# The second MLP's output product with w_out stationary and 512 tokens moving, its rows brought back by block transposes and a DRAM tile, and an earlier first plan

## The chip, the cores and the metric

One core of a Trainium2 chip. The metric is the device time of one execution in microseconds (us). TensorE is called PE here, VectorE DVE, ScalarE ACT, GpSimd POOL, and SyncE, whose only work is DMA, SP.

## What is computed

Attention with squared ReLU, times u; then a mixture of 8 experts in which each token goes to one; then a second MLP with ELU. Sizes: 8 x 3072 tokens of 256; expert hidden width 1024; hidden width of the second MLP 2048.

```python
scores = (1.0 / S) * np.matmul(z, z.transpose(0, 2, 1))
x = (u * np.matmul(np.maximum(scores, 0.0) ** 2, v)).reshape(B * S, D)
# experts
xn, en = x / norm(x), expert_emb / norm(expert_emb)
logits = xn @ en.T / tau
expert_idx, gate_w = argmax(logits, axis=1), softmax(logits) at that index
for e in range(E):
    mask = expert_idx == e
    out[mask] = gate_w[mask, None] * (np.maximum(x[mask] @ w1[e], 0.0) @ w2[e])
# second MLP, on these rows
h = x @ w_in
g = np.where(h > 0.0, h, np.exp(np.minimum(h, 0.0)) - 1.0)
return (g @ w_out).astype(np.float32)
```

## The kernel before

Each operand of a product is held as two numbers, hi and lo (a rounded part and the rest). A product is hi by hi, hi by lo and lo by hi, three matmuls for one.

**Stages.** A list of steps runs over the whole program. Its first 576 are attention: 48 chunks of 512 queries, 12 steps each. Behind them come units: A (one tile of 512 tokens of one expert, 4 steps, 41 of them), B (a rest tile of 256 tokens, 2 steps, 21), M (the second MLP on the tile of an A, 8 steps, 41), and D (the second MLP on 512 of the rows that the B units left, 8 steps, 7, the last of them by functions of its own, l_h and l_acc). Their order is A0, A1, M0, A2, M1, ... M5, then A6, B0, M6, A7, B1, M7, ..., then the remaining A and M, then D0 to D6.

**The loop over steps** (from L1343) writes for step n: its first product h on PE, the DVE operations d1 to d4 of step n - 1 with at most one planned task between two of them, the list `pre[n]` (among others the PE transposes of the next unit's rows, L852), the second product acc of step n - 2 on PE (LAG is 2), g of step n on ACT, and then the rest of the tasks planned for n. An engine runs what is written for it in that order. Tasks are placed by `at(step, task)` and `spread(tasks, first, last)`, which chooses steps by a running sum of each engine's costs.

**Buffers.** PSUM has two tiles for first products (pss, from t_ps) and two for sums (psa, from t_acc). 48 equal slots in SBUF, tag "g", hold nearly all tiles, in turn.

**The second product of M and D** is m_acc: the 128 x 128 pieces of hi and lo of g are stationary, and w_out moves: 512 wide (its hi and lo side by side) for hi, 256 wide for lo. A step has 16 matmuls. The sum of a unit takes both psa tiles, [tokens, hi-part | lo-part] for four quarters of 128 tokens. The last step goes by halves of the tokens; behind each half ACT copies the two parts to o2 and o. m_out then adds them on DVE (in-place in o) and scatters four times 128 rows to the output by the token numbers in ids, planned by the lines at L1336 to L1338.

**Attention's second product**, att_acc, is written the other way: v is stationary, 512 queries move, and psa holds the transposed result. evac_ops brings it back: a DVE transpose of 32 x 32 blocks from PSUM into xt (the columns of v are permuted by the host for that, in layout), four writes to a DRAM tile xr, one read from it as rows x.

**The plan.** route_ops counts the tokens of each expert by groups of two chunks and scatters token numbers into the table tok on POOL. plan1 works out which expert and which place in tok the first 6 A tiles have, when the group g1 (L1279) is through; plan2 does it for the rest, when all are. From those numbers POOL gathers for each unit ids from tok, then the rows of x by ids, and the weights wst by the expert.

Of the kernel before, what the change touches and what calls it, by code (L numbers as in the profile page):

```python
# [17 lines left out]
LAG = 2  # L18
# [10 lines left out]
def attn_moe_mlp(ctx, tc, zT, u, v, emb, tau, wp, w_in, w_out, out):  # L29
# [23 lines left out]

    xs = dr.tile([N, D], F32, name="xs")
    xr = dr.tile([N, D], F32, name="xr")
    tok = dr.tile([E * N, 1], I32, name="tok")
    dn = dr.tile([NR, D], F32, name="dn")
    dnid = dr.tile([NR, 1], I32, name="dnid")
# [41 lines left out]
    def cp(o, a):  # L100
        act.activation(out=o, in_=a, func=AF.Copy)  # L101
# [298 lines left out]
        tt(lo, r, f(hi), ALU.subtract)  # L400
        HL[C, m] = [hi, lo]

    def att_acc(C, m):

        if m == 0:
            AC[C] = t_acc()
        hi, lo = HL.pop((C, m))
        vt = V[C // NC, m]
        for part in range(2):
            for dc in range(2):  # L410
                a = AC[C][:, dc]
                for j in range(2):
                    vh, vl = (vt[:, j, o + dc * 128:o + dc * 128 + 128] for o in (0, 256))
                    if part == 0:
                        mm(a, vh, hi[:, j], m == 0 == j, False)
                        mm(a, vl, hi[:, j], False, False)
                    else:
                        mm(a, vh, lo[:, j], False, m == CS - 1 and j == 1)

    def evac_ops(C):  # L420

        g, o = chunk_group[C]
        h = {}
        rows = xr[C * 512:(C + 1) * 512, :]

        def tr():
            h["t"] = slot("xt", F32, (16, 2, 32))
            vec.transpose(out=h["t"], in_=AC.pop(C).rearrange("p a (b r) -> p b a r", r=32))

        def put():  # L430
            for i in range(4):
                sp.dma_start(rows.rearrange("(b r) d -> r b d", r=32)[:, :, i * 64:(i + 1) * 64],
                             h["t"][i * 32:(i + 1) * 32].rearrange("p b a c -> p b (a c)"))

        def get():
            X[C] = slot("x", F32, (4, 256))
            sp.dma_start(X[C], rows.rearrange("(t p) d -> p t d", p=128))

        def mul():
            if o == 0:  # L440
                n2t[g] = sb.tile([128, MAXT], F32, name="n2", tag="n2", bufs=3)
                dott[g] = sb.tile([128, MAXT, E], F32, name="dot", tag="dot", bufs=3)
            tt(X[C], X[C], UT.pop(C), ALU.mult)

        def sq(q):
            def fn():
                act.activation(out=K["junka"], in_=X[C][:, q], func=AF.Square,
                               accum_out=n2t[g][:, o + q:o + q + 1])
            return fn
        return tr, put, get, mul, [sq(q) for q in range(4)]  # L450
# [370 lines left out]
    def rows_ops(key):  # L821
        kind, j = key
        nt = 4 if kind == "A" else 2

        def idx(t):
            if kind == "A":
                return K["ixa"][:, j, t:t + 1] if j < NA1 else K["ixb"][:, j - NA1, t:t + 1]
            return K["ixB"][:, j, t:t + 1]
        h = {}

        def gi(t):
            def fn():
                if t == 0:
                    IDS[key] = sb.tile([128, 4], I32, name="ids", tag="ids", bufs=6)
                    h["x"] = slot("rows", F32, (4, 256))
                gather(IDS[key][:, t:t + 1], tok[:, :], idx(t), E * N - 1)
            return fn

        def gx(t):
            def fn():  # L840
                gather(h["x"][:, t], xs[:, :], IDS[key][:, t:t + 1], N - 1)
            return fn
        return [gi(t) for t in range(nt)] + [gx(t) for t in range(nt)], h
# [46 lines left out]

    def a_acc(key, i):
        if i == 0:
            AC[key] = [t_acc()[:, 0] for _ in range(2)]
        hi, lo = HL.pop((key, i))
        w = W2[key, i]
        last = i == 3
        for dc in range(2):
            a = AC[key][dc]
            for g in range(2):
                sl = slice(g * 256 + dc * 128, g * 256 + dc * 128 + 128)  # L900
                mm(a, w[:, 0, sl], hi[:, g], i == 0 and g == 0, False)
# [27 lines left out]
                scatter(dn[:, :], x[:, t], iv, NR - 1)  # L929

    PR = set()

    def m_r(key, i):
        p, e, y = PS[key, i]
# [42 lines left out]
    def l_acc(key, i):  # L977
# [14 lines left out]
                    mm(a[:, q, :256], lo[:, j, c], w[:, g, :256], False, st)  # L992
        if last:
            if hf == 0:
                PS[key] = slot("o", F32, (4, 256)), None
            o = PS[key][0][:, 2 * hf:2 * hf + 2]
            cp(o, a[:, :, 256:])
            tt(o, o, a[:, :, :256], ALU.add)
            for fn in m_out(key)[1 + 2 * hf:3 + 2 * hf]:
                fn()  # L1000

    def m_g(key, i):
        p, e, y = PS[key, i]
# [24 lines left out]

    def m_acc(key, i):
        if i == 0:  # L1030
            AC[key] = [t_acc(), t_acc()]
        hi, lo = HL.pop((key, i))
        w = WO[i]
        last = i == NF2 // 2 - 1
        for qs in ((0, 1), (2, 3)) if last else ((0, 1, 2, 3),):
            for part in range(2):
                for q in qs:
                    a = AC[key][q // 2][:, q % 2]
                    sl = slice(q * 128, q * 128 + 128)
                    for j in range(2):  # L1040
                        st = last and j == 1
                        if part == 0:
                            mm(a, hi[:, j, sl], w[:, j], i == 0 and j == 0, st)
                        else:
                            mm(a[:, :256], lo[:, j, sl], w[:, j, :256], False, st)
            if last:
                q = qs[1]
                if q == 1:
                    PS[key] = slot("o", F32, (4, 256)), slot("o2", F32, (4, 256))
                o, t = PS[key]  # L1050
                ap = AC[key][q // 2]
                cp(t[:, q - 1:q + 1], ap[:, :, 256:])
                cp(o[:, q - 1:q + 1], ap[:, :, :256])

    def m_out(key):
        def add():
            o, t = PS[key]
            tt(o, o, t, ALU.add)

        def sc(q):  # L1060
            def fn():
                ids = IDS["A", key[1]] if key[0] == "M" else IDS[key]
                scatter(out[:, :], PS[key][0][:, q], ids[:, q:q + 1], N - 1)
            return fn
        return [add] + [sc(q) for q in range(4)]

    def d_prep(key):
        h = {}

        def ld():  # L1070
            h["x"] = slot("xd", F32, (4, 256))
            IDS[key] = sb.tile([128, 4], I32, name="ids", tag="ids", bufs=6)
            j = key[1]
            sp.dma_start(h["x"], dn[j * 512:(j + 1) * 512, :].rearrange("(t p) d -> p t d", p=128))
            sp.dma_start(IDS[key], dnid[j * 512:(j + 1) * 512, :].rearrange("(t p) o -> p (t o)", p=128))
# [200 lines left out]
        route_end[g] = w  # L1276

    at(CS, plan_const)
    g1 = chunk_group[(B - 1) * NC + 1][0]  # L1279
    w = route_end[g1]  # L1280
    spread(plan1_ops(), w + 1, w + 6, 0.2)
    p1 = w + 6
# [16 lines left out]
    for un in units:  # L1299
# [34 lines left out]
            at(n - 5, dl)  # L1334
            pre[n - 2] += do
        if k in "MD" and un != units[-1]:  # L1336
            w = n + nst[k] + LAG + (2 if k == "D" else 0)
            spread(m_out(un), w, w + 2)  # L1338

    def emit(n, k):  # L1340
        if 0 <= n < len(steps):
# [21 lines left out]
def layout(u, v, z, emb, tau, w1, w2, w_in, w_out):  # L1363
# [2 lines left out]
    E, D, F = w1.shape  # L1366
    c = np.ascontiguousarray

    B, S, _ = v.shape
    vp = v.reshape(B, S, 4, 2, 32).transpose(0, 1, 3, 2, 4).reshape(B, S, D)  # L1370
    w1p = w1.reshape(E, 2, 128, F)
    w2p = w2.reshape(E, F // 128, 128, D).transpose(0, 2, 1, 3)
    return {
# [1 line left out]
        "tau": c(np.asarray(tau).reshape(1)),  # L1375
        "wp0": c(w1p[:, 0].reshape(E * 128, F)), "wp1": c(w1p[:, 1].reshape(E * 128, F)),
        "wp2": c(w2p[:, :, 0:4].reshape(E * 128, 4 * D)), "wp3": c(w2p[:, :, 4:8].reshape(E * 128, 4 * D)),
        "w_in": c(w_in).view(np.int64), "w_out": c(w_out).view(np.int64),
    }


# [15 lines left out]
```

## Time and profile before

| | us |
|---|---|
| median of 3 runs | 5435.11 |
| lowest, highest | 5433.26, 5435.74 |
| the profiled execution | 5439.36 |
| its span in the profile | 5437.4 |

The profile shows one execution. Its page gives the busy time of each engine over the span; the rows further below are from its trace. A row of the timeline is: start in us, busy time in us, engine, line, operation, the tile written and the tiles read, shape, number of instructions in the row; in brackets the idle time of the engine before it and what ended that. Busy times of matmuls overlap, so the spacing of starts is what a stream costs. A releaser is inferred from semaphores: of several it is the one that came last.

### The profile page before, as it was taken

Reading aid. Unit: us, or ns where it says so; the run is one execution under the profiler, and the core shown is the slowest. Engines: PE = TensorE matmul, PEld = TensorE weight load, DVE = VectorE, ACT = ScalarE, POOL = GpSimd, SP = SyncE. Lnnn points to the kernel's source line nnn. Section 1 sums busy time; section 2 is a strip of 40 time slices with the busy share of each in tenths; the row PEclk is TensorE's granted clock in tenths of the full one; section 3 lists DMA queues with packets and bytes.
Section 4 is the critical chain, followed back from the end, with each engine's and each line's share of the span. In section 5 each row is a group of like instructions: output and inputs, shape, how many; then the busy total and the mean of one; then the engine's idle time right before and its main releaser. Section 6 shows DMA issues by size and latency. Waiting matters only on the chain. (4 is left out here: it accounts for less than half of the span.)

```text
span 5437.4 us, 72993 instructions
## 1 busy us (share of the span) xinstructions
PE 5403.8 (99%) x26532; PEld 4566.6 (84%) x26532; DVE 4187.9 (77%) x7839; ACT 4082.3 (75%) x4762; POOL 1382.3 (25%) x1207
## 2 busy tenths in 40 slices
PE   9999999999999999999999999999999999999998
PEld 7888888888888887888888888888888888888887
DVE  8888888888888877887677667767766777777887
ACT  7989988898999885667666666666665666666776
POOL 0011101111110104324444344434444222221011
PEclk9999999999999999999999999999999999999999
DMA  3333323332333314102222222222222111110000
GB/s 112 84 79 87 83 79 86 70 90 78 82 86 83 79 53 155 55 28 74 76 68 82 65 82 66 82 68 75 74 74 70 39 52 49 48 48 27 20 24 20
DMA packets 303063, 374.11 MB, mean 69 GB/s; under 512 B 136492, under 2 KB 244527, under 8 KB 302704
## 3 DMA queue, kind: packets, MB, share of 16 engines
q0 software_dynamic: 76896, 206.62, 12.4%
q1 hardware_dynamic: 225808, 162.84, 11.6%
q8 instruction: 209, 3.42, 0.3%
q14 instruction: 150, 1.23, 0.1%
HBM read 266.72 MB, written 92.39 MB: 66 GB/s over the span
## 5 line engine op out<-in xcount | busy, mean ns | idle before, releaser
L104 PE MATMUL psa<-hi,v 128*128 128x512 f32 x4608 | 1143.8, 390 | 0.0
L104 PEld LDWEIGHTS psa<-hi,v 128*128 128x128 f32 x4608 | 865.3, 188 | 179.6 <-DVE hi L391 0.9
L83 DVE TENSOR_TENSOR lo<-r,hi 128x1024 fp32r<-128x1024 f32 x576 | 705.0, 1224 | 243.0 <-ACT hi L101 237.6
L104 PE MATMUL pss<-x2h,wi 128*128 128x512 f32 x2624 | 814.1, 391 | 0.0
L104 PE MATMUL psa<-wo,hi 128*128 128x512 f32 x3072 | 780.8, 392 | 0.6 <-DVE hi L1020 0.6
L93 DVE SCALAR_TENSOR_TENSOR y<-e,y 128x1024 f32<-128x1024 f32 x384 | 469.6, 1223 | 378.7 <-ACT e L1005 375.1
L370 ACT ACTIVATE r<-pss 128x1024 f32<-128x1024 f32 x576 | 591.1, 1026 | 207.1 <-PE pss L104 203.9
L952 ACT ACTIVATE e<-pss 128x1024 f32<-128x1024 f32 x376 | 386.5, 1028 | 430.2 <-PE pss L104 426.3
L104 PEld LDWEIGHTS psa<-wo,hi 128*128 128x128 f32 x3072 | 570.9, 188 | 115.3 <-DVE hi L1020 0.9
L375 ACT ACTIVATE r<-r 128x1024 f32<-128x1024 f32 x576 | 611.6, 1062 | 18.3
L577 POOL DMA_INDIRECT tok<-idt,pi x192 | 226.5, 1179 | 1566.0 <-DVE pi L556 860.4
L104 PE MATMUL psa<-lo,v 128*128 128x512 f32 x2304 | 615.9, 389 | 0.0
L788 POOL DMA_INDIRECT out<-o,ids x192 | 206.1, 1074 | 1567.8 <-ACT hi L879 558.2
L95 DVE SCALAR_TENSOR_TENSOR junk<-x,en 128x256 f32<-128x256 f32 x1536 | 599.8, 416 | 0.0
L879 ACT ACTIVATE hi<-pss 128x1024 fp32r<-128x1024 f32 x206 | 211.9, 1029 | 495.8 <-PE pss L104 495.8
L104 PEld LDWEIGHTS pss<-x2h,wi 128*128 128x128 f32 x2624 | 476.5, 189 | 86.4
L104 PE MATMUL pss<-x2l,wi 128*128 128x512 f32 x1312 | 510.5, 389 | 0.0
L104 PEld LDWEIGHTS psa<-lo,v 128*128 128x128 f32 x2304 | 432.7, 188 | 90.0
L101 ACT ACTIVATE hi<-r 128x1024 fp32r<-128x1024 f32 x460 | 488.3, 1062 | 14.6
L83 DVE TENSOR_TENSOR y<-r,y 128x1024 f32<-128x1024 f32 x384 | 470.6, 1225 | 33.2 <-DVE y L93 0.5
L83 DVE TENSOR_TENSOR lo<-y,hi 128x1024 fp32r<-128x1024 f32 x384 | 470.5, 1225 | 17.8
L104 PE MATMUL pss<-zp 128*128 128x512 f32 x1152 | 450.5, 391 | 14.0 <-ACT r L370 7.6
(166 smaller groups left out, 9915.7 us busy)
## 6 DMA issues: line engine op xcount, KB each, us to landing
vs<-v SPq DMA_DIRECT2D x48, 512.0 KB, 6.1
u<-u SPq DMA_DIRECT2D x48, 512.0 KB, 6.0
xr<-xt SPq DMA_DIRECT2D x192, 128.0 KB, 2.6
x<-xr SPq DMA_DIRECT2D x48, 512.0 KB, 4.9
xs<-x SPq DMA_DIRECT2D x48, 512.0 KB, 4.8
zz<-zT SPq DMA_DIRECT2D x46, 256.0 KB, 5.8
zq<-zp POOLq DMA_DIRECT2D x46, 256.0 KB, 3.9
w<-w_in SPq DMA_DIRECT2D x8, 512.0 KB, 4.3
```

Source lines behind the costliest of these rows:

```text
L83: vec.tensor_tensor(out=o, in0=a, in1=b, op=op)
L93: vec.scalar_tensor_tensor(out=o, in0=a, scalar=s, in1=b, op0=op0, op1=op1)
L95: vec.scalar_tensor_tensor(out=o, in0=a, scalar=s, in1=b, op0=op0, op1=op1, accum_out=acc)
L101: act.activation(out=o, in_=a, func=AF.Copy)
L104: pe.matmul(o, lhsT=l, rhs=r, start=start, stop=stop, skip_group_check=True)
L370: act.activation(out=r, in_=p, func=AF.Relu, scale=1.0 / S)
L375: act.activation(out=r, in_=r, func=AF.Square)
L577: pool.indirect_dma_start(out=tok[:, :], out_offset=bass.IndirectOffsetOnAxis(ap=h["pi"][:, t:t + 1], axis=0), in_=K["idt"][:, gt:gt + 1], ...
L788: pool.indirect_dma_start(out=dst, out_offset=bass.IndirectOffsetOnAxis(ap=idx, axis=0), in_=src, in_offset=None, bounds_check=bound, oob_ ...
L879: act.activation(out=hi, in_=p, func=AF.Relu)
L952: act.activation(out=e, in_=p, func=AF.Relu, scale=-1.0)
```

## The change

1. m_acc uses vw_acc, the former body of att_acc: w_out stationary, 512 tokens moving, 8 matmuls with hi and 4 with lo in a step, all 512 wide, and one psa tile for a unit in place of two. No split of the last step.
2. m_out is replaced by out_ops: the transpose, the four writes and the read of evac_ops (now rows_by_dram) with a new DRAM tile orow, then the four scatters. For a unit that starts at step n and has 8 steps: transpose in step n + 9, writes n + 10, read n + 11, scatters from n + 13 to n + 15. The ids live longer and get 8 buffers in place of 6.
3. The columns of w_out are permuted by the host as those of v are. l_acc, the last D unit's, undoes that with permuted views in its copies and additions, now by quarters of the tokens.
4. a_acc takes one psa tile where it took halves of two.
5. g1 is the group of chunk 41, not of chunk 43: plan1 goes from steps 561 to 566 into 537 to 542.

```diff
@@ -53,6 +53,7 @@
 
     xs = dr.tile([N, D], F32, name="xs")
     xr = dr.tile([N, D], F32, name="xr")
+    orow = dr.tile([N, D], F32, name="orow")
     tok = dr.tile([E * N, 1], I32, name="tok")
     dn = dr.tile([NR, D], F32, name="dn")
     dnid = dr.tile([NR, 1], I32, name="dnid")
@@ -400,32 +401,25 @@
         tt(lo, r, f(hi), ALU.subtract)
         HL[C, m] = [hi, lo]
 
-    def att_acc(C, m):
-
-        if m == 0:
-            AC[C] = t_acc()
-        hi, lo = HL.pop((C, m))
-        vt = V[C // NC, m]
+    def vw_acc(a, w, hi, lo, first, last):
+
         for part in range(2):
             for dc in range(2):
-                a = AC[C][:, dc]
                 for j in range(2):
-                    vh, vl = (vt[:, j, o + dc * 128:o + dc * 128 + 128] for o in (0, 256))
+                    wh, wl = (w[:, j, o + dc * 128:o + dc * 128 + 128] for o in (0, 256))
                     if part == 0:
-                        mm(a, vh, hi[:, j], m == 0 == j, False)
-                        mm(a, vl, hi[:, j], False, False)
+                        mm(a[:, dc], wh, hi[:, j], first and j == 0, False)
+                        mm(a[:, dc], wl, hi[:, j], False, False)
                     else:
-                        mm(a, vh, lo[:, j], False, m == CS - 1 and j == 1)
-
-    def evac_ops(C):
-
-        g, o = chunk_group[C]
+                        mm(a[:, dc], wh, lo[:, j], False, last and j == 1)
+
+    def rows_by_dram(rows, acc, get_tile):
+
         h = {}
-        rows = xr[C * 512:(C + 1) * 512, :]
 
         def tr():
             h["t"] = slot("xt", F32, (16, 2, 32))
-            vec.transpose(out=h["t"], in_=AC.pop(C).rearrange("p a (b r) -> p b a r", r=32))
+            vec.transpose(out=h["t"], in_=acc().rearrange("p a (b r) -> p b a r", r=32))
 
         def put():
             for i in range(4):
@@ -433,8 +427,21 @@
                              h["t"][i * 32:(i + 1) * 32].rearrange("p b a c -> p b (a c)"))
 
         def get():
+            sp.dma_start(get_tile(), rows.rearrange("(t p) d -> p t d", p=128))
+        return tr, put, get
+
+    def att_acc(C, m):
+        if m == 0:
+            AC[C] = t_acc()
+        vw_acc(AC[C], V[C // NC, m], *HL.pop((C, m)), m == 0, m == CS - 1)
+
+    def evac_ops(C):
+
+        g, o = chunk_group[C]
+        def x_tile():
             X[C] = slot("x", F32, (4, 256))
-            sp.dma_start(X[C], rows.rearrange("(t p) d -> p t d", p=128))
+            return X[C]
+        tr, put, get = rows_by_dram(xr[C * 512:(C + 1) * 512, :], lambda: AC.pop(C), x_tile)
 
         def mul():
             if o == 0:
@@ -831,7 +838,7 @@
         def gi(t):
             def fn():
                 if t == 0:
-                    IDS[key] = sb.tile([128, 4], I32, name="ids", tag="ids", bufs=6)
+                    IDS[key] = sb.tile([128, 4], I32, name="ids", tag="ids", bufs=8)
                     h["x"] = slot("rows", F32, (4, 256))
                 gather(IDS[key][:, t:t + 1], tok[:, :], idx(t), E * N - 1)
             return fn
@@ -890,12 +897,12 @@
 
     def a_acc(key, i):
         if i == 0:
-            AC[key] = [t_acc()[:, 0] for _ in range(2)]
+            AC[key] = t_acc()
         hi, lo = HL.pop((key, i))
         w = W2[key, i]
         last = i == 3
         for dc in range(2):
-            a = AC[key][dc]
+            a = AC[key][:, dc]
             for g in range(2):
                 sl = slice(g * 256 + dc * 128, g * 256 + dc * 128 + 128)
                 mm(a, w[:, 0, sl], hi[:, g], i == 0 and g == 0, False)
@@ -929,6 +936,7 @@
                 scatter(dn[:, :], x[:, t], iv, NR - 1)
 
     PR = set()
+    OUTS = {}
 
     def m_r(key, i):
         p, e, y = PS[key, i]
@@ -992,12 +1000,13 @@
                     mm(a[:, q, :256], lo[:, j, c], w[:, g, :256], False, st)
         if last:
             if hf == 0:
-                PS[key] = slot("o", F32, (4, 256)), None
-            o = PS[key][0][:, 2 * hf:2 * hf + 2]
-            cp(o, a[:, :, 256:])
-            tt(o, o, a[:, :, :256], ALU.add)
-            for fn in m_out(key)[1 + 2 * hf:3 + 2 * hf]:
-                fn()
+                PS[key] = slot("o", F32, (4, 256))
+            for q in range(2):
+                o = PS[key][:, 2 * hf + q]
+                ov = o.rearrange("p (i b c) -> p b i c", i=4, b=2)
+                cp(ov, a[:, q, 256:].rearrange("p (b i c) -> p b i c", i=4, b=2))
+                tt(ov, ov, a[:, q, :256].rearrange("p (b i c) -> p b i c", i=4, b=2), ALU.add)
+                scatter(out[:, :], o, IDS[key][:, 2 * hf + q:2 * hf + q + 1], N - 1)
 
     def m_g(key, i):
         p, e, y = PS[key, i]
@@ -1028,48 +1037,31 @@
 
     def m_acc(key, i):
         if i == 0:
-            AC[key] = [t_acc(), t_acc()]
-        hi, lo = HL.pop((key, i))
-        w = WO[i]
-        last = i == NF2 // 2 - 1
-        for qs in ((0, 1), (2, 3)) if last else ((0, 1, 2, 3),):
-            for part in range(2):
-                for q in qs:
-                    a = AC[key][q // 2][:, q % 2]
-                    sl = slice(q * 128, q * 128 + 128)
-                    for j in range(2):
-                        st = last and j == 1
-                        if part == 0:
-                            mm(a, hi[:, j, sl], w[:, j], i == 0 and j == 0, st)
-                        else:
-                            mm(a[:, :256], lo[:, j, sl], w[:, j, :256], False, st)
-            if last:
-                q = qs[1]
-                if q == 1:
-                    PS[key] = slot("o", F32, (4, 256)), slot("o2", F32, (4, 256))
-                o, t = PS[key]
-                ap = AC[key][q // 2]
-                cp(t[:, q - 1:q + 1], ap[:, :, 256:])
-                cp(o[:, q - 1:q + 1], ap[:, :, :256])
-
-    def m_out(key):
-        def add():
-            o, t = PS[key]
-            tt(o, o, t, ALU.add)
+            AC[key] = t_acc()
+        vw_acc(AC[key], WO[i], *HL.pop((key, i)), i == 0, i == NF2 // 2 - 1)
+
+    def out_ops(key):
+
+        i = OUTS.setdefault(key, len(OUTS))
+        h = {}
+
+        def tile_():
+            h["o"] = slot("o", F32, (4, 256))
+            return h["o"]
 
         def sc(q):
             def fn():
                 ids = IDS["A", key[1]] if key[0] == "M" else IDS[key]
-                scatter(out[:, :], PS[key][0][:, q], ids[:, q:q + 1], N - 1)
-            return fn
-        return [add] + [sc(q) for q in range(4)]
+                scatter(out[:, :], h["o"][:, q], ids[:, q:q + 1], N - 1)
+            return fn
+        return rows_by_dram(orow[i * 512:(i + 1) * 512, :], lambda: AC.pop(key), tile_) + tuple(sc(q) for q in range(4))
 
     def d_prep(key):
         h = {}
 
         def ld():
             h["x"] = slot("xd", F32, (4, 256))
-            IDS[key] = sb.tile([128, 4], I32, name="ids", tag="ids", bufs=6)
+            IDS[key] = sb.tile([128, 4], I32, name="ids", tag="ids", bufs=8)
             j = key[1]
             sp.dma_start(h["x"], dn[j * 512:(j + 1) * 512, :].rearrange("(t p) d -> p t d", p=128))
             sp.dma_start(IDS[key], dnid[j * 512:(j + 1) * 512, :].rearrange("(t p) o -> p (t o)", p=128))
@@ -1276,7 +1268,7 @@
         route_end[g] = w
 
     at(CS, plan_const)
-    g1 = chunk_group[(B - 1) * NC + 1][0]
+    g1 = chunk_group[(B - 1) * NC - 1][0]
     w = route_end[g1]
     spread(plan1_ops(), w + 1, w + 6, 0.2)
     p1 = w + 6
@@ -1334,8 +1326,12 @@
             at(n - 5, dl)
             pre[n - 2] += do
         if k in "MD" and un != units[-1]:
-            w = n + nst[k] + LAG + (2 if k == "D" else 0)
-            spread(m_out(un), w, w + 2)
+            w = n + nst[k] + LAG - 1
+            tr, put, get, *sc = out_ops(un)
+            at(w, tr)
+            at(w + 1, put)
+            at(w + 2, get)
+            spread(sc, w + 4, w + 6)
 
     def emit(n, k):
         if 0 <= n < len(steps):
@@ -1366,8 +1362,7 @@
     E, D, F = w1.shape
     c = np.ascontiguousarray
 
-    B, S, _ = v.shape
-    vp = v.reshape(B, S, 4, 2, 32).transpose(0, 1, 3, 2, 4).reshape(B, S, D)
+    vp, op = (t.reshape(-1, 4, 2, 32).transpose(0, 2, 1, 3).reshape(t.shape) for t in (v, w_out))
     w1p = w1.reshape(E, 2, 128, F)
     w2p = w2.reshape(E, F // 128, 128, D).transpose(0, 2, 1, 3)
     return {
@@ -1375,7 +1370,7 @@
         "tau": c(np.asarray(tau).reshape(1)),
         "wp0": c(w1p[:, 0].reshape(E * 128, F)), "wp1": c(w1p[:, 1].reshape(E * 128, F)),
         "wp2": c(w2p[:, :, 0:4].reshape(E * 128, 4 * D)), "wp3": c(w2p[:, :, 4:8].reshape(E * 128, 4 * D)),
-        "w_in": c(w_in).view(np.int64), "w_out": c(w_out).view(np.int64),
+        "w_in": c(w_in).view(np.int64), "w_out": c(op).view(np.int64),
     }
 
 
```

On PE, inside an M unit, a step of before (psa is the sum, pss the first product, wo and wi are w_out and w_in, x2h and x2l the expert's rows in two parts):

```order
L104 MATMUL pss<-x2l,wi 128x512
L104 MATMUL psa<-wo,hi 128x512 x8
L104 MATMUL psa<-wo,lo 128x256 x8
L104 MATMUL pss<-x2h,wi 128x512 x2
L104 MATMUL pss<-x2l,wi 128x512
```

and the same place now:

```order
L105 MATMUL pss<-x2l,wi 128x512
L105 MATMUL psa<-hi,wo 128x512 x8
L105 MATMUL psa<-lo,wo 128x512 x4
L105 MATMUL pss<-x2h,wi 128x512 x2
L105 MATMUL pss<-x2l,wi 128x512
```

Eight matmuls of 256 have become four of 512; the first product around them stands as it did.

On DVE, from the last step of an M unit into the A unit behind it (lo from pss and hi is the A unit's, one a step; w is a part of a weight, xb the rows of the next B tile, o the output rows), before:

```order
L83 TENSOR_TENSOR lo<-y,hi 128x1024
L93 SCALAR_TENSOR_TENSOR lo<-pss,hi 128x1024
L83 TENSOR_TENSOR w<-wst,w 128x512 x3
L93 SCALAR_TENSOR_TENSOR lo<-pss,hi 128x1024
L83 TENSOR_TENSOR w<-wst,w 128x512
L83 TENSOR_TENSOR xb<-pss,xb 128x512
L83 TENSOR_TENSOR o<-o,o_37142 128x1024
L93 SCALAR_TENSOR_TENSOR lo<-pss,hi 128x1024
```

and now:

```order
L84 TENSOR_TENSOR lo<-y,hi 128x1024
L94 SCALAR_TENSOR_TENSOR lo<-pss,hi 128x1024
L84 TENSOR_TENSOR w<-wst,w 128x512 x3
L422 STREAM_TRANSPOSE xt<-psa 128x1024
L94 SCALAR_TENSOR_TENSOR lo<-pss,hi 128x1024
L84 TENSOR_TENSOR w<-wst,w 128x512
L84 TENSOR_TENSOR xb<-pss,xb 128x512
L94 SCALAR_TENSOR_TENSOR lo<-pss,hi 128x1024
```

The transpose stands ahead of the A unit's second lo, where the addition stood two operations behind it.

On POOL, around the last eight scatters of token numbers (tok; ids, rows and wst are the gathers for one A unit, out the scatters of M's output rows), before:

```order
L788 DMA out<-o,ids 24576x256
L783 DMA wst<-wp,wia 128x1024
L788 DMA out<-o,ids 24576x256
L783 DMA wst<-wp,wia 128x1024 x2
L577 DMA tok<-idt,pi 196608x1 x8
L783 DMA ids<-tok,ixa 128x1 x4
L783 DMA rows<-xs,ids 128x256 x4
```

and now:

```order
L790 DMA rows<-xs,ids 128x256 x4
L790 DMA wst<-wp,wia 128x1024 x4
L584 DMA tok<-idt,pi 196608x1 x8
L795 DMA out<-o,ids 24576x256 x4
L790 DMA ids<-tok,ixa 128x1 x4
L790 DMA rows<-xs,ids 128x256 x4
```

The output scatters, which stood between the weight gathers, stand behind the token scatters.

## Rows read from the trace of the kernel before

**Rows 1.** Windows: start:end, length, busy of PE, PEld, DVE, ACT, POOL, clock, DMA, GB/s

```profile
2300.00:5200.00 2900.00, 2900.00 (x15171) 2488.40 (x15170) 2108.87 (x2210) 1949.72 (x2287) 1018.89 (x852) 1.00 0.19 60
...
2090.00:2100.00 10.00, 8.43 (x25) 6.51 (x26) 8.70 (x15) 9.91 (x17) 8.02 (x7) 0.64 0.28 92
2260.00:2270.00 10.00, 9.96 (x47) 8.44 (x48) 7.27 (x8) 4.87 (x5) 0.00 (x0) 0.83 0.00 0
```

**Rows 2.** Timeline of PE, one unit of eight D steps

```profile
5024.24 1.98 PE L104 MATMUL psa<-wo,hi 128*128 128x512 f32 x8
5026.06 1.12 PE L104 MATMUL psa<-wo,lo 128*128 128x256 f32 x8
5027.01 0.63 PE L104 MATMUL pss<-x2h,wi 128*128 128x512 f32 x2
...
5057.32 1.98 PE L104 MATMUL psa<-wo,hi 128*128 128x512 f32 x8
...
5068.38 1.98 PE L104 MATMUL psa<-wo,hi 128*128 128x512 f32 x8
```

**Rows 3.** Timeline of PE, A steps: first matmul of h, and five steps later

```profile
2128.35 0.62 PE L104 MATMUL pss<-xh,w 128*128 128x512 f32 x2
...
2155.55 0.62 PE L104 MATMUL pss<-x2h,wi 128*128 128x512 f32 x2
```

**Rows 4.** Groups by line and shape, DVE: count, busy us, mean ns, idle before

```profile
L428 DVE STREAM_TRANSPOSE xt<-psa 128x1024 f32<-128x1024 f32 x48 | 59.9, 1249 | 83.2 <-PE psa L104 83.1
L83 DVE TENSOR_TENSOR o<-o,o 128x1024 f32<-128x1024 f32 x47 | 57.2, 1216 | 0.0
```

**Rows 5.** DMA issues of the page: queue, count, KB each, us to landing

```profile
xr<-xt SPq DMA_DIRECT2D x192, 128.0 KB, 2.6
x<-xr SPq DMA_DIRECT2D x48, 512.0 KB, 4.9
```

**Rows 6.** Timeline of DVE, PE and ACT, an A unit behind M, B next

```profile
3389.39 1.23 DVE L93 SCALAR_TENSOR_TENSOR lo<-pss,hi 128x1024 fp32r<-128x1024 f32 x1 [1.36 <-ACT hi L879]
...
3390.91 0.63 PE L104 MATMUL pss<-xh,w 128*128 128x512 f32 x2
...
3391.11 1.09 ACT L101 ACTIVATE o<-psa 128x512 f32<-128x512 f32 x2 [0.31 <-PE psa L104]
...
3393.69 0.46 PE L852 MATMUL pss<-ident,rows 128*128 128x128 f32 x4
```

**Rows 7.** Timeline of DVE and POOL at the last eight token scatters

```profile
2286.22 0.17 DVE L556 CAST pi<-sm 128x8 int32<-128x8 f32 x1
...
2299.59 1.34 POOL L577 DMA_INDIRECT tok<-idt,pi  x1 [0.30 <-issue]
...
2335.11 1.73 POOL L783 DMA_INDIRECT ids<-tok,ixa  x1 [3.56 <-DMA tok<-idt,pi]
...
2335.96 0.70 DVE L1020 CAST hi<-y 128x1024 fp32r<-128x1024 f32 x1
```

**Rows 8.** Timeline of POOL, ACT and PE where the stages meet

```profile
2071.80 1.06 POOL L783 DMA_INDIRECT ids<-tok,ixa  x1 [4.98 <-DVE junk L95]
...
2088.01 0.63 ACT L101 ACTIVATE w<-wst 128x512 fp32r<-128x512 f32 x1 [10.77 <-DMA wst<-wp,wia]
...
2091.57 0.80 PE L104 MATMUL pss<-zp 128*128 128x512 f32 x1 [7.61 <-ACT r L370]
...
2260.04 0.88 PE L852 MATMUL pss<-ident,rows 128*128 128x128 f32 x8 [1.96 <-ACT r L937]
```

**Rows 9.** Timeline of POOL and DVE at the end

```profile
5399.11 1.21 POOL L788 DMA_INDIRECT out<-o,ids  x1 [34.62 <-ACT r L937]
...
5403.79 0.69 DVE L83 TENSOR_TENSOR o<-o,psa 128x512 f32<-128x512 f32 x1 [0.93 <-ACT o L101]
...
5416.14 0.97 POOL L788 DMA_INDIRECT out<-o,ids  x1 [1.70 <-DMA out<-o,ids]
...
5424.06 0.97 POOL L788 DMA_INDIRECT out<-o,ids  x1 [6.95 <-DVE o L83]
```

## The prediction

> **What bounds the kernel now.** I read the table of windows first: from 2300 to 5200 us, the stage of the experts and of the second MLP, PE is busy for 2900.00 of 2900.00 us at a granted clock of 1.00 (2.4 GHz), while DVE has 2108.87 and ACT 1949.72 us of work [rows 1]. So there the time is what PE issues, and anything else matters only if it makes PE wait. Second, PE's timeline, for the distance between the starts of two pieces of its stream; busy durations overlap and can't be added. Third, the timelines of DVE, ACT and POOL at the few places where PE is closest to a wait. PE did wait where the stages meet: 7.61 us before 2091.57 and 1.96 us before 2260.04 [rows 8], each followed by a stretch of low clock (0.64 and 0.83 [rows 1]).
>
> **The stream of PE in an M or D unit.** One of the 8 steps has 12 matmuls of h, 512 wide, then in m_acc 8 with hi, 512 wide, and 8 with lo, 256 wide [rows 2]. In numbers of that piece: 5026.06 - 5024.24 = 1.82 us for the eight hi, 5027.01 - 5026.06 = 0.95 us for the eight lo, and the rest of the step for h. Six steps last 5057.32 - 5024.24 = 33.08 us, 5.513 each, and the unit of eight 5068.38 - 5024.24 = 44.14 us; its last step, cut in two halves of tokens, is only a little longer.
> After: 8 hi and 4 lo, all 512 wide. The columns are the same (8 x 256 = 4 x 512); four issues fewer. The row nearest to the new step is an A step, which has 12 matmuls of h and 12 of the second product, all 512 wide and with the weights stationary, as the new m_acc has them: five such steps last 2155.55 - 2128.35 = 27.20 us, 5.440 each [rows 3]. The new unit is thus 8 x 5.440 = 43.52 us, and the saving 44.14 - 43.52 = 0.62 us a unit. There are 41 M units and 7 D units, of which the last keeps its own path (l_acc): 47 x 0.62 = **29.1 us**, all of it on the path that sets the end. Bounds: 0, if the new step took 5.513 like the old, and 29.1; I take the A steps, since operand form, width and count are equal. Where the 0.62 lies: by the A steps a matmul of 512 columns is 5.440/24 = 0.2267 us, so in each old step the lo pairs are 0.95 - 4 x 0.2267 = 0.043 too long (four pairs, 11 ns each, 1504 pairs, 16 us in all), and h and hi together 5.513 - 0.95 - 20 x 0.2267 = 0.03; eight such steps are 0.58, the split of the last step the remaining 0.04.
>
> A rule bears on this. The Trainium skill, "TensorE: Matmul & The Clock Gate", section "Back-to-back issue gap", gives an isolated matmul of N columns at the full clock N/2.4 ns plus 2.5 ns. By it two matmuls of 256 cost only 2.5 ns more than one of 512, and my estimate from that page is 1504 x 2.5 = 3.8 us instead of 29.1. The trace's 11 ns a pair, and its steps, speak against it; the case is a rival below, with a price from rows.
>
> **The evacuation.** Gone per unit: four ACT copies from PSUM and a DVE addition (1.216 us, 47 of them [rows 4]). New: one DVE transpose from PSUM, for which the attention's of the same shape is the row (1.249 us [rows 4]). DVE's work is equal within 0.03 us a unit, ACT's falls; neither engine sets the end [rows 1]. The detour over DRAM adds, per unit, four writes of 128 KB and a read of 512 KB, in attention 2.6 and 4.9 us to landing [rows 5]. They are issued by SP a step apart; the four scatters come two steps behind the read, 2 x 5.44 = 10.9 us against 4.9. Behind them on POOL stand gathers for tiles several steps ahead. On SP the read stands ahead of the D units' loads, which are made five steps early. Cost 0; without that cover POOL would hold its queue for the rest of a landing, at most 4.9 us, still less than a step. IDS gets 8 buffers for the longer life of the ids.
>
> **The transpose at the head of the A units.** This is the new dependence I looked at most. In the order of DVE the transpose stands ahead of the second lo(A). In before, lo(A) of the first step runs at 3389.39 for 1.23 us, and PE's transposes for the B tile (L852), which want the PSUM buffer that lo(A) reads, start at 3393.69 [rows 6]: 3.07 us of margin. After, DVE first waits for the end of m_acc's last step: in before the next matmul starts at 3390.91 and ACT's copy 0.20 us later, at 3391.11 [rows 6]. With m_acc 0.06 shorter the transpose would run from 3391.05 to 3392.30, lo(A) directly behind it to about 3393.45, and PE wants the buffer at about 3393.6. A margin of 0.1 to 0.2 us, in each of the 21 places where A, B and M follow one another. Bounds: 0, and 0.3 us each (the two operations without any overlap and a hand-over of 0.20 between them and to PE: 3391.05 + 1.25 + 0.20 + 1.23 + 0.20 = 3393.93): 6.3 us. I take 0.5 us in total, as the times close without a wait.
>
> **M1 and the token scatters.** On POOL M1's four output scatters stood ahead of the last group's eight token scatters; now they stand behind. In before these run from 2299.59 to 2335.11, 35.5 us, though their index was written at 2286.22 already [rows 7]; now they may start as soon as that is there and the four weight gathers are issued. If they start at 2286.4 the outputs go at about 2322 to 2334, if at 2299.6 at 2335 to 2347. The slot of that o tile is used again by a hi (2335.96 [rows 7]), on which PE depends about 4 us later. Bounds 0 and 4 us, once; I take 0.5.
>
> **The earlier plan.** The six first A tiles are planned 24 steps earlier, from 42 chunks. But the stall between the stages ends with a transfer: ACT's w waits 10.77 us for the weight gather and PE 7.61 us for ACT's r behind it [rows 8]. On POOL the eight token scatters of group 21 still stand ahead of the ids gather (2071.80 [rows 8]), and that gather still reads the token table, so it waits for the last of them to land; row and weight gathers follow as before. The row names a DVE operation (junk) as releaser, but by the code the ids gather needs of DVE only its index tile, which plan1 wrote steps earlier. I take 0; the bounds are 0 and the whole stall, 7.61 us plus the low clock behind it, 10 x (1 - 0.64) = 3.6 us: 11.2 us gained.
>
> **The tail.** In before D5's four scatters and the first pair of the last unit are six, from 5399.11 to 5416.14, 3.41 us apart; the last pair goes at 5424.06, as its o is done [rows 9]. Now the first pair goes first (its o is done at 5403.79 + 0.69 [rows 9]), then D5's four: six scatters to 5404.5 + 6 x 3.41 = 5425.0 in the old frame, 0.9 later than 5424.06; at 2.7 us apart no delay, at 3.9 apart 3.8. Each token quarter's o is scattered by itself, which may gain 0.5. Bounds -0.5 and +3.8; I take +0.5.
>
> **Sum:** -29.1 + 0.5 + 0.5 + 0 + 0.5 = **-27.6 us**. The profiled execution took 5439.36 us; with the change 5411.8. The median of three runs is 4.2 us below it, 5435.11; with the change **5407.5 us** (-0.5%).
>
> **Rivals.**
> *Part of it comes back.* The margin of A's lo is negative (6.3 us), and M1's slot (4) and the tail (3.8) go towards their upper bounds: 5435.11 - 29.1 + 6.3 = 5412 with the first alone, 5420 with all. For it: margins of 0.1 us in 21 places. Against it: PE follows DVE and ACT closely elsewhere, with a window of 2900 us without idle time [rows 1].
> *The stall between the stages shrinks.* Then 11.2 us more go: 5407.5 - 11.2 = 5396.3. For it: plan operations leave DVE just there. Against it: the transfer chain above.
> *The change does not do what it says for PE.* The surcharge isn't the narrow matmul's but something that stays (the switch between operands, the first reading of hi). Then the step stays at 5.513 us, the 29.1 us are not there and the terms above add 1.5: 5435.11 + 1.5 = 5436.6, no change. Against it: the A steps [rows 3]. The Trainium skill's rule cited above would give the same case with 3.8 us less, 5432.8.
> *Slower.* lo(A) behind the transpose makes PE wait long enough in each of the 21 places for the clock to fall, as the wait of 1.96 us before 2260.04 did [rows 8], which was followed by 10 us at 0.83, 1.7 us lost [rows 1]. 21 x (1.96 + 1.7) = 77 us against 27.6: 5435.11 - 27.6 + 77 = 5484. It decides from 27.6/21 = 1.3 us per place, wait and clock together, which is a DVE delayed by about one more operation of 1.2 us than I count.
>
> **Chances.** Forecast 0.61, part of it comes back 0.17, smaller stall 0.09, no change 0.08, slower 0.05. A measurement of this kernel can tell about 0.2%, 11 us, from no change: forecast, part and smaller stall are beyond that, faster 0.87, same 0.08, slower 0.05. The range reaches from 5399 (a third of the stall gone beside the sum) to 5423 (the upper end of the part that comes back, 5420, and the 2.5 us by which the runs before differ): it leaves out the whole stall gone, no change and slower, 0.22 in all, with a little of the stall's case inside.
>
> **What would show it.** Right: in a unit in the late D stage the start-to-start of a step is 5.44 us and of a unit 43.5; the matmul rows lose the 256-wide lo of m_acc; 48 + 47 transposes of about 1.25 us; DVE's additions of 128x1024 o are gone; PE's waits still hold about 7.6 us for r and 2 us at the second place, and nothing new of over 10 us in sum. Wrong: steps of 5.5 us (the surcharge stays); PE waiting for DVE's lo at the L852 transposes 21 times; a clock below 1.00 in windows of the A, B, M cycles; POOL waiting for reads of x rows' kind for steps; a stall between the stages shorter or longer than before.

## The result, and the profile after

The changed kernel takes 5486.86 us (median of 4 runs, 5481.33 to 5488.64), the kernel before 5435.42 us in the same comparison: a ratio of 1.0093, 95% interval 1.0076 to 1.0111. It is 51 us slower (41 to 60 by the interval), where 28 us faster was forecast.

The first part of the page (busy us of each engine, share of the span, instructions), of the kernel before and then, with its span, of the changed kernel; the span before is 5437.4 us:

```profile
PE 5403.8 (99%) x26532; PEld 4566.6 (84%) x26532; DVE 4187.9 (77%) x7839; ACT 4082.3 (75%) x4762; POOL 1382.3 (25%) x1207
```

```profile
span 5479.4 us, 70218 instructions
...
PE 5385.4 (98%) x25028; PEld 4483.5 (82%) x25028; DVE 4189.4 (76%) x7841; ACT 3982.2 (73%) x4576; POOL 1404.0 (26%) x1207
```

1504 matmuls are gone, and PE has less to do over the whole span, yet the span is longer. So PE waits. The table of windows for the stretch of [rows 1] says how long (length, then busy time of PE, PEld, DVE, ACT, POOL, clock, DMA share, GB/s):

```profile
2300.00:5200.00 2900.00, 2841.16 (x13655) 2380.24 (x13654) 2069.66 (x2175) 1830.46 (x2094) 1036.86 (x849) 1.00 0.24 73
```

2841.16 of 2900 us where before it was all of them, at a clock of 1.00: idle time of PE, not a slower PE. PE's longest waits (engine, line, tile, what it waited for: us in total, times, longest), before and then in the changed kernel:

```profile
PE pss L104 <- ACT r L370: 7.6, 1, 7.6
PE pss L104 <- DVE zp L83: 5.6, 1, 5.6
PE pss L852 <- ACT r L937: 2.0, 1, 2.0
```

```profile
PE psa L105 <- DVE x2l L84: 63.5, 41, 2.0
PE pss L105 <- DVE zp L84: 5.7, 1, 5.7
PE pss L105 <- ACT r L371: 3.2, 1, 3.2
PE pss L859 <- ACT r L945: 2.0, 1, 2.0
```

41 waits of 1.5 us on average, one for each A unit, of a kind that the kernel before has not got: a matmul into psa waits for DVE's x2l. One of them, on the timelines of PE, DVE and ACT of the changed kernel (start, busy, instruction; in brackets the idle time before it and what ended it):

```profile
5063.95 0.61 PE L105 MATMUL psa<-hi,w 128*128 128x512 f32 x2
5064.40 0.39 PE L105 MATMUL psa<-lo,w 128*128 128x512 f32 x1
...
5066.47 0.72 PE L105 MATMUL psa<-hi,w 128*128 128x512 f32 x2 [1.68 <-DVE x2l L84]
...
5064.59 1.23 DVE L84 TENSOR_TENSOR lo<-y,hi 128x1024 fp32r<-128x1024 f32 x1
5065.73 0.68 DVE L84 TENSOR_TENSOR x2l<-psa,x2h 128x512 fp32r<-128x512 f32 x1
...
5064.83 0.60 ACT L102 ACTIVATE x2h<-psa 128x512 fp32r<-128x512 f32 x1 [0.33 <-PE psa L105]
```

This is the last of the four steps of the last A unit. a_acc finishes the first half of the 256 output columns (the matmuls of 5063.95 and 5064.40 are its last), ACT and DVE split that half into x2h and x2l, and PE should go on with the second half. In the kernel before the second half lies in another psa tile. Change 4 put both halves into one, and PE's next matmul into that tile stands behind the reads of its first half: ACT's x2h, 0.60 us, then DVE's x2l, which has to let a lo of 1.23 us end first. The next matmul starts at 5066.47 instead of about 5064.63 (the spacing of 0.2267 us behind the one at 5064.40).

The wait is not the chip's choice, it is in the program. The order of PE's instructions with the waits that each carries, in the changed kernel, at the middle of such a step (DVE_49 is the semaphore that DVE's operations raise):

```
4751 L105 MATMUL psa<-hi,w 128x512 x2
4752 L105 MATMUL psa<-lo,w 128x512
4753 L105 MATMUL psa<-hi,w 128x512 [waits DVE_49]
4754 L105 MATMUL psa<-hi,w 128x512
```

The first half ends at 4752, and 4753, the first matmul of the second half, waits for DVE.

### The profile page after: what moved, and what is told of

It reads as the page before. It is cut to its first block, busy times and chain, and to the rows that moved or that the text cites. A ratio compares the mean times of both kernels' runs of the same rounds, so it can differ in the third digit from the quotient of the medians.

```text
span 5479.4 us, 70218 instructions
## 1 busy us (share of the span) xinstructions
PE 5385.4 (98%) x25028; PEld 4483.5 (82%) x25028; DVE 4189.4 (76%) x7841; ACT 3982.2 (73%) x4576; POOL 1404.0 (26%) x1207
## 3 DMA queue, kind: packets, MB, share of 16 engines
q14 instruction: 153, 1.25, 0.1%
## 5 line engine op out<-in xcount | busy, mean ns | idle before, releaser
L105 PE MATMUL psa<-hi,wo 128*128 128x512 f32 x3008 | 749.1, 391 | 0.0
L105 PEld LDWEIGHTS psa<-hi,wo 128*128 128x128 f32 x3008 | 562.1, 188 | 115.0
L105 PEld LDWEIGHTS pss<-x2h,wi 128*128 128x128 f32 x2624 | 489.9, 188 | 99.9
L105 PE MATMUL psa<-hi,w 128*128 128x512 f32 x1312 | 412.1, 395 | 63.5 <-DVE x2l L84 63.5
```

What stands on the lines that cost most here:

```text
L105: pe.matmul(o, lhsT=l, rhs=r, start=start, stop=stop, skip_group_check=True)
```

## The experiments

### Two tiles again

```diff
         if i == 0:
-            AC[key] = t_acc()
+            AC[key] = [t_acc()[:, 0] for _ in range(2)]
...
         for dc in range(2):
-            a = AC[key][:, dc]
+            a = AC[key][dc]
```

> The changed kernel, with one edit: a_acc takes halves of two psa tiles again, as in the kernel before. Theory (one tile for both halves of the A unit's sum: PE's matmuls of the second half wait until ACT and DVE have read the first half, 41 times some 1.8 us): the 41 waits of PE for x2l (63.5 us of idle time in the changed kernel) are gone and the time is 5435.4 - 29.1 (PE's stream in M and D) - 4.4 (the shorter stall between the stages in the changed kernel's trace) = 5402, between 5398 and 5410. Rival (the transpose ahead of the A unit's second lo, or the longer way of the rows over DRAM, is what costs): the time stays above 5450, and PE's waits move to another releaser.

Measured: 5410.75 us against 5439.41 us of the kernel before, a ratio of 0.9947, interval 0.9933 to 0.9961. With one edit the change is 28.7 us faster than the kernel before instead of 51 us slower. PE's waits in this kernel, all of 1 us and more in total:

```profile
PE pss L105 <- ACT r L371: 6.5, 1, 6.5
PE pss L105 <- DVE zp L84: 5.7, 1, 5.7
PE pss L859 <- ACT r L945: 2.0, 1, 2.0
PE psa L105 <- DVE lo L84: 1.5, 2, 0.8
PE pss L105 <- DVE lo L94: 1.0, 2, 0.8
```

No x2l among them. The same place in the A unit before the last, on the timelines of PE, DVE and ACT of this kernel:

```profile
4929.53 0.39 PE L105 MATMUL psa<-lo,w 128*128 128x512 f32 x1
4929.76 0.62 PE L105 MATMUL psa<-hi,w 128*128 128x512 f32 x2
...
4930.94 0.69 DVE L84 TENSOR_TENSOR x2l<-psa,x2h 128x512 fp32r<-128x512 f32 x1
...
4929.96 0.60 ACT L102 ACTIVATE x2h<-psa 128x512 fp32r<-128x512 f32 x1 [0.33 <-PE psa L105]
```

ACT and DVE read the first half from 4929.96 to 4931.63 while PE goes on with the second from 4929.76. The reads cost the same as in the changed kernel; only PE isn't held by them. The time lies 0.75 us above the expected range (5398 to 5410) and 8.75 us above the expected 5402. Of these, 4.4 us are the stall between the stages, which is 6.5 us here and not 3.24, of which more below; 4.0 us are the kernel before, 5439.41 us beside these runs and 5435.42 beside the first ones.

### The kernel before with one tile

```diff
         if i == 0:
-            AC[key] = [t_acc()[:, 0] for _ in range(2)]
+            AC[key] = t_acc()
...
         for dc in range(2):
-            a = AC[key][dc]
+            a = AC[key][:, dc]
```

> The kernel before, with one edit: a_acc takes one psa tile for both halves of its sum. Theory: PE waits for x2l 41 times here too, 1.55 us each and some 0.3 us of start-up, 41 x 1.85 = 76 us: about 5511, between 5490 and 5525. Rival (the wait needs the new second product beside it): within 15 us of 5435.

Measured: 5512.22 us, a ratio of 1.0135 (1.0117 to 1.0154), 73 us slower. Its wait:

```profile
PE psa L104 <- DVE x2l L83: 63.1, 41, 1.9
```

The wait needs nothing of the new second product: 41 times, 63.1 us here and 63.5 us in the changed kernel. What one of them costs, start to start, is more than PE's idle time. Between the PE transposes of the rows of two successive A units, where one A and one M lie between, of the kernel with one tile added to it, of the changed kernel and of the one with two tiles:

```profile
4569.60 0.81 PE L852 MATMUL pss<-ident,rows 128*128 128x128 f32 x8
4638.24 0.79 PE L852 MATMUL pss<-ident,rows 128*128 128x128 f32 x8
```

```profile
4548.01 0.79 PE L859 MATMUL pss<-ident,rows 128*128 128x128 f32 x8
4616.02 0.80 PE L859 MATMUL pss<-ident,rows 128*128 128x128 f32 x8
```

```profile
4559.41 0.79 PE L859 MATMUL pss<-ident,rows 128*128 128x128 f32 x8
4625.44 0.80 PE L859 MATMUL pss<-ident,rows 128*128 128x128 f32 x8
```

68.64, 68.01 and 66.03 us: the changed kernel loses 68.01 - 66.03 = 1.98 us a cycle, 0.3 us more than the idle time of 1.68 (0.72 us for the first two matmuls instead of 0.61, and the time between the next start that the spacing gives and the end of the last matmul, from where idle time is counted). In the kernel before the same cycle is 4979.66 - 4913.01 = 66.65 us, so its one tile costs it 1.99. In the 21 cycles with a B unit the same measure, over A, B and M, is 79.75 against 78.05 us, 1.7 us. 20 x 1.98 + 21 x 1.7 = 75 us.

### Both halves read after the matmuls of both

```diff
-            if last:
-                if dc == 0:
-                    X2[key] = rslot("x2h"), rslot("x2l")
-                split(X2[key][0][:, dc], X2[key][1][:, dc], a)
+        if last:
+            X2[key] = rslot("x2h"), rslot("x2l")
+            for dc in range(2):
+                split(X2[key][0][:, dc], X2[key][1][:, dc], AC[key][:, dc])
```

> The changed kernel, one psa tile in a_acc, but ACT and DVE read both halves only after the matmuls of both. Theory: no matmul of A waits for x2l any more; in the 20 places where A and M lie 4 or more steps apart nothing else waits, in the 21 places A, B, M the first product of M stands directly behind A's last matmul and waits for x2h and x2l, 1 to 2 us each: PE waits 20 to 45 us in all, the time 5425 to 5450, between the changed kernel and the one with two tiles. Rival (the cause is not in the two halves of one tile): 5480 or more.

Measured: 5437.70 us, a ratio of 0.9998 (0.9988 to 1.0008), between the other two as expected. The one wait of over 1 us in total that it adds to those of the kernel with two tiles, less idle time than the 20 to 45 us expected:

```profile
PE pss L105 <- ACT x2h L102: 14.4, 21, 0.7
```

One psa tile is not the cost by itself; the read between the two halves is. Read late, the 41 waits are gone, and in the 21 places where M stands directly behind its A and B the first product of M waits for x2h: 0.69 us of idle time each, and the cycle is 79.3 us against 78.05, 1.25 us each, 26 us in all. A part that the idle time does not show is a second hold: in one of these places the matmul that reads x2l starts at 3415.77, just behind the end of DVE's x2l at 3415.72. So reading half of the sum early pays, and for that the halves have to be separate tiles here.

### The earlier plan alone

```diff
-    g1 = chunk_group[(B - 1) * NC + 1][0]
+    g1 = chunk_group[(B - 1) * NC - 1][0]
```

> The kernel before with the earlier plan alone (42 chunks in place of 44). Theory (plan1's DVE operations out of the last attention steps bring the last routing and the ids gather forward, since PE's wait between the stages fell from 7.61 to 3.24 us in the changed kernel): that wait is 3 to 4 us here too, the time 5430 to 5432. Rival (as predicted: the stall is the token scatters' and gathers' and varies from run to run): the wait is 7 to 8 us, or anything, with tok spacings alone different, 5435.

Measured: 5436.46 us, a ratio of 0.9996 (0.9987 to 1.0005): no difference. PE's wait there:

```profile
PE pss L104 <- ACT r L370: 6.3, 1, 6.3
```

The expected 3 to 4 us did not show. The wait is 7.61 us in [rows 8], 6.3 us here, 6.5 us with two tiles, 6.9 us in a second profile of the changed kernel, and 3.2 us in its first. In that first profile the last token scatter was issued at 2060.80, 4 to 5 us earlier than here (2064.94) and with two tiles (2065.65), while the first of the eight started within about 1 us of theirs. What the first profile gained lies in the spacing of that run's token scatters, each of which waits for the landing of the one before it; what made them land sooner is open.

### The weight gathers ahead of the token scatters

On the kernel with two tiles:

```diff
             for o in wl:
-                at(w, o, 2)
+                at(w - 11 if un == ("A", 0) else w, o, 2)
```

> e1_two_acc, and the first A unit's four weight gathers are planned 11 steps earlier, which the earlier plan allows: on POOL they stand ahead of the last eight token scatters of attention's end instead of behind ids and rows. Theory (the stall between the stages ends with the landing of the weight gathers, and the earlier plan does nothing as long as they stand behind the scatters): ACT no longer waits some 10 us for wst, PE's wait of 6.5 us for r and the stretch of low clock behind it are gone, 8 to 12 us less than e1_two_acc: a ratio to the kernel before of 0.9925 to 0.9933. Rival (something else is late there at the same time, such as the rows or a slot): the wait moves to another releaser and at most 3 us are gained.

Measured: 5401.65 us, a ratio of 0.9933 (0.992 to 0.9947) to the kernel before, 37 us faster and 8 us more than with two tiles alone. The intervals of the two ratios overlap, so the 8 us rest on the traces, which differ at the expected place. The table of windows from 2080 to 2100 us, where the stall lies, of the kernel with two tiles and then of this one:

```profile
2080.00:2090.00 10.00, 3.48 (x16) 2.59 (x15) 1.86 (x3) 2.43 (x4) 7.56 (x9) 0.78 0.69 229
2090.00:2100.00 10.00, 10.00 (x32) 7.75 (x33) 9.21 (x21) 9.90 (x17) 7.88 (x6) 0.71 0.17 49
```

```profile
2080.00:2090.00 10.00, 10.00 (x45) 8.28 (x45) 9.73 (x23) 9.60 (x17) 8.17 (x7) 1.00 0.15 42
2090.00:2100.00 10.00, 10.00 (x50) 8.31 (x49) 9.62 (x21) 6.10 (x11) 7.26 (x7) 1.00 0.21 58
```

And this kernel's timelines of POOL and ACT:

```profile
2007.33 1.07 POOL L790 DMA_INDIRECT wst<-wp,wia  x1 [25.64 <-PE psa L105]
...
2066.44 1.45 POOL L584 DMA_INDIRECT tok<-idt,pi  x1 [4.29 <-DMA tok<-idt,pi]
...
2076.57 1.13 ACT L102 ACTIVATE w<-wst 128x512 fp32r<-128x512 f32 x2
```

ACT's w no longer waits (10.77 us in [rows 8]), PE doesn't idle, and the clock stays at 1.00 where it was 0.78 and 0.71 (0.64 in [rows 1]). The stall did end with the weight gathers, and it ended late because they stood behind the scatters on POOL. The earlier plan is what allows the gathers to go ahead of them: by the code they now stand in step 556, behind plan1's new end (542) and ahead of its old one (566). By itself the earlier plan moves nothing.

### The width of the lo matmuls

On the kernel with two tiles, m_acc alone:

```diff
-                        mm(a[:, dc], wh, lo[:, j], False, last and j == 1)
+                        for s in ((slice(0, 256), slice(256, 512)) if cut else (slice(0, 512),)):
+                            mm(a[:, dc, s], wh, lo[:, j, s], False, last and j == 1)
...
-        vw_acc(AC[key], WO[i], *HL.pop((key, i)), i == 0, i == NF2 // 2 - 1)
+        vw_acc(AC[key], WO[i], *HL.pop((key, i)), i == 0, i == NF2 // 2 - 1, True)
```

> The kernel with two psa tiles in a_acc (e1_two_acc), and the 4 lo matmuls of 512 in a step of M and D cut into 8 of 256, each with the same stationary piece of w_out: the issues of the kernel before, in the operand form of the changed one. Theory (the saving comes from fewer, wider issues): 4 pairs a step cost 11 ns each more, and h behind a 256-wide matmul starts 0.03 us later: 0.05 to 0.07 us a step, 47 x 8 = 376 steps, 18 to 27 us more than e1_two_acc, a ratio to the kernel before of 0.9978 to 0.9997. Rival (the saving comes from the operand form, w_out stationary and g moving): within 5 us of e1_two_acc, a ratio of 0.994 to 0.9955.

Measured: 5438.19 us, a ratio of 0.9999 (0.999 to 1.0009): the whole gain is gone, a little more than the 18 to 27 us expected. PE's timeline in M39, the unit of [rows 2] too (an M unit, not a D unit as its heading has it), of the kernel with two tiles and then of this one:

```profile
5005.32 1.98 PE L105 MATMUL psa<-hi,wo 128*128 128x512 f32 x8
5007.13 1.07 PE L105 MATMUL psa<-lo,wo 128*128 128x512 f32 x4
5008.04 0.61 PE L105 MATMUL pss<-x2h,wi 128*128 128x512 f32 x2
...
5010.76 1.98 PE L105 MATMUL psa<-hi,wo 128*128 128x512 f32 x8
```

```profile
5024.86 1.98 PE L105 MATMUL psa<-hi,wo 128*128 128x512 f32 x8
5026.67 1.11 PE L105 MATMUL psa<-lo,wo 128*128 128x256 f32 x8
5027.62 0.63 PE L105 MATMUL pss<-x2h,wi 128*128 128x512 f32 x2
...
5030.37 1.98 PE L105 MATMUL psa<-hi,wo 128*128 128x512 f32 x8
```

A step is 5.44 us with 512-wide lo and 5.51 us with 256-wide, where eight of 256 take 0.95 us and four of 512 take 0.91, and h behind them 2.75 instead of 2.72. So the saving comes from fewer, wider issues and not from the operand form: with w_out stationary and 256 tokens moving the step is as long as in [rows 2], where the tokens were stationary. An issue brings its own weight load (x26532 and x25028 for PE and PEld alike on the two pages), so number of issues, width and weight loads change together, and no run here parts them.

### The changed kernel once more

> The changed kernel as it is, timed beside the kernel before on one chip, to see whether the parts add up. By them: -29.1 us for PE's stream, +73 us for the 41 waits (the 72.8 us by which e2_before_one_acc was slower), nothing for the plan: 44 us more than the kernel before, a ratio of 1.0081. Rival (a part is still missing, since 5486.86 to 5435.42 us were 51 us): a ratio of 1.0093 or more, and a wait in the trace that e1_two_acc and e2_before_one_acc have not.

Measured: 5488.18 us against 5438.33, a ratio of 1.0091 (1.0074 to 1.0108), 50 us slower; PE's waits again 63.5 us for x2l and 6.9 us for r, and none that the others have not. That is 6 us more than the sum that was expected. By spans, the second profile has 5485.7 us and the kernel with two tiles 5408.7: 77 us, of which the cycles above account for 75. The sum of the expectation took the 73 us of the kernel before with one tile, which is 4 less than the 77; the intervals of these ratios, some 10 us to either side, are wider than that.

## Why the prediction was wrong

**What bounds the kernel** was read rightly: PE's stream, and whatever makes PE wait.

**The stream of M and D** was right in mechanism and size. The A steps of [rows 3] gave 5.440 us; the new step is 5010.76 - 5005.32 = 5.44, and the cycle of one A and one M is 66.03 us with two tiles where it was 66.65, the 0.62 us a unit that were forecast. The kernel with two tiles is 28.7 us faster, the sum said 27.6. The rule of the Trainium skill, "TensorE: Matmul & The Clock Gate", section "Back-to-back issue gap", for an isolated matmul, from which 3.8 us were estimated, was rightly left aside: the cut to 256 shows 28 us for these 1504 issues, some 18 ns each, not 2.5.

**The step that failed** is one that the prediction does not contain. It went through the change by the second product, the evacuation, the transpose's place, POOL, the plan and the tail; point 4 of the change, a_acc with one psa tile, has no term in the sum, not even a zero with its cover named. It gives no reason for leaving it out; the halves, their matmuls and their reads are the same, so that it looks like a matter of names. But the cover of the reads of the first half was PE's work on the second half in another tile. With one tile, the next write waits for the reads before it: 1.7 to 2.0 us, 41 times, 75 us in place of nothing, two and a half times the gain. The order of instructions without the waits shows no difference there, and the trace of before could not show a wait that wasn't in it; the rows that price it were there. On the timelines of PE, ACT and DVE of the kernel before, in the last step of the last A unit, PE's start of the second half and the two reads of the first:

```profile
5020.16 0.62 PE L104 MATMUL psa<-hi,w 128*128 128x512 f32 x2
...
5020.36 0.60 ACT L101 ACTIVATE x2h<-psa 128x512 fp32r<-128x512 f32 x1 [0.33 <-PE psa L104]
...
5021.27 0.68 DVE L83 TENSOR_TENSOR x2l<-psa,x2h 128x512 fp32r<-128x512 f32 x1
```

The reads end at 5021.27 + 0.68 = 5021.95. A second half that has to stand behind them starts 1.8 us later than 5020.16, and 41 x 1.8 = 73 us could have been a term, or a rival.

**The rival on the other side** had the right sign and nearly the right size (77 us, 5484) for the wrong reason. It put the wait at lo(A) behind the transpose, 21 times, with the clock falling. In the kernel with two tiles that place shows what was worked out, on PE's and DVE's timelines:

```profile
3379.97 0.62 PE L105 MATMUL pss<-xh,w 128*128 128x512 f32 x2
...
3382.69 0.46 PE L859 MATMUL pss<-ident,rows 128*128 128x128 f32 x4
...
3380.17 1.25 DVE L422 STREAM_TRANSPOSE xt<-psa 128x1024 f32<-128x1024 f32 x1 [2.87 <-PE psa L105]
3381.34 1.18 DVE L94 SCALAR_TENSOR_TENSOR lo<-pss,hi 128x1024 fp32r<-128x1024 f32 x1
```

The transpose starts 0.20 us behind the start of the next matmul, as it was put, lo ends at 3382.52 and PE goes on at 3382.69: a margin of 0.17 us, inside the 0.1 to 0.2 given, and no wait. And in the changed kernel the clock from 2300 to 5200 us was 1.00, though 38 of its 41 waits lie there.

**The other terms.** The detour over DRAM cost PE nothing, with landings of 2.5 and 3.9 us. M1's scatters: the token scatters began at 2284.96 and M1's four outputs went from 2316.40 to 2327.44 in the kernel with two tiles, and no wait of PE shows there: 0 for the 0.5 taken. The tail: from PE's last matmul to the last scatter 5398.02 - 5393.42 = 4.60 us with two tiles and 5426.74 - 5422.16 = 4.58 before, so 0 of the 0.5. The earlier plan: 0, as said; the weight gathers are what the stall ends with, and the price of 11.2 us for the whole stall was some 8 us when it was lifted.

## What to carry to other kernels

When two halves of a sum move into one tile, look for a read of the first half that stands between the writes of the two: the matmuls and the reads stay as they are, and still the writer now waits for the reader. Give every edit of a change its term, also one that only renames where a result lies, and compare the waits in the order of instructions as well as the instructions. Two kernels that differ in one such line tell more than the sum of a change with five parts: here a gain of 29 us and a loss of 75 us lay in the same diff.

## What the hardware showed that was not expected

PE's clock stayed at 1.00 over 2900 us in which PE idled 38 times for 1.4 to 2.0 us, while one idle time of 1.96 us was followed by a window of 0.83 [rows 1, 8]. The same wait of 1.96 us stands in every kernel here, and what follows it differs even between two profiles of one: 0.84 in the first of the changed kernel, 1.00 in the second, and 1.00 in the kernel with only the earlier plan. An idle time of 2 us may or may not be followed by a low clock, and no run here tells which. Each of the 41 waits cost 0.3 us beyond its idle time (1.98 us for 1.68, and 1.7 for 1.41).

Whether PE could write the second half of a tile while the first is read, without the wait, was not tried.
